# Scores and carried product on 64x64 quarters, and one written order for two stages, in a recurrent-attention and two-layer kernel

## The chip, the cores and the metric

One core of a Trainium2 chip runs the whole computation. The metric is device time in microseconds, the median of several executions of one program. Times inside an execution come from one profiled execution. Engines are called as the profile calls them: PE (matmul), PEld (weight load), DVE (vector), ACT (scalar), POOL, and SP, which here only issues DMAs.

## What is computed

Thirty-two heads (4 batches of 8) run a gated linear recurrence over 768 steps, and two dense layers follow on 3072 tokens.

```
for t in range(768):                                   # head dim 48
    state = alpha[:, :, t, :, None] * state + k[t] (outer) v[t]
    y[t]  = q[t] @ state
x   = y as (3072, 384)
h   = x @ w1_in ; x = max(0.01*h, h) @ w1_out          # d_ff 2048
h   = x @ w2_in ; out = elu(h) @ w2_out
```

## The kernel before

**Units.** The recurrence is cut into chunks of 128 steps. A unit is one chunk of one batch, all 8 heads as 4 pairs; there are 24, six in a row (c = u % 6) for each batch. The two heads of a pair lie at partitions 0 to 47 and 64 to 111. A unit makes, on PE in fp32 (each such product stands as two instructions in the trace): the scores `sc` (`attn_sc`, L171, lhsT of 48 rows by 128 columns, one bank for each half of the pairs), the transposed keys `pk` (L179), the output `po` from masked scores and values (L225, 128 rows by 64 or 48 columns), the carried product added to the same `po` (L231: the state `T`, 48 by 48, against the queries, only when c > 0), and the state update `pu` (L244, when c < 5). DVE masks the scores (L193), prepares keys and queries by two scans (`prep_k`, `prep_F`, `prep_q`), and adds the state (L268). `po` is then split in a high part `xh` (ACT, L250) and a low part `xl` (DVE, L253) of the x tile of a block.

**Blocks.** Four units make a block of 512 tokens. The fourth pair of a unit is spread over the free partitions of the other three pairs by six DMAs of 64 KiB on SP's queue (`gather`, L282) before the block can be used by layer 1. There are 6 blocks, and each of the two layers goes over 16 steps m for a block. A step is nine matmuls of `hp` (128x512, in a PSUM bank of `ps_h`, two banks), an activation on ACT and DVE, a split of the result in `gh` (ACT) and `gl` (DVE), and nine matmuls into `y` or `o`. The loop over `seq` issues, in step s, first `hp` of step s+2 (LA = 2) and its activation, then pieces of attention, then `y` of step s. `gh` and `gl` have two buffers, so that `gh` of step s+2 has to wait for the `y` of step s.

**Attention under layer 1.** Units 0 to 7 and the first heads of blocks 0 and 1 have an order written out by hand, up to step 16 (`in_order` ties each engine's instructions to program order). From there units 8 to 23 are handed out as pieces (`pieces`, four indices for a unit, index 0 `sc` and `pk`, index 1 the preparation of the next unit, index 2 `po` and `pu`) so that a block is complete in time for the next block of layer 1. From there on the order on each engine is the scheduler's (`behind` only keeps it after the part ordered by hand). After a unit's last piece the pack and values of unit u+3 are loaded by two DMAs of 674 and 288 KiB on ACT's queue (L116, L128).

**Layer 2's weights.** They come as 8-byte words and are converted in place over layer 1's weights by 32 conversions of four DVE and three ACT instructions (L290 to L302). All of them are asked for in the 16 steps of layer 1's last block. In layer 2, `guard_load` and `guard_unit` read the decay factors of every unit once more, and check on ACT that they are in range (L590, L594, L595).

`ps_a` has three banks that `sc` (two), `pk`, `po` and `pu` take in turn.

Of the kernel before, what the change touches and what calls it, by code (L numbers as in the profile page):

```python
# [19 lines left out]
def attention_two_layers_kernel(  # L20
# [17 lines left out]
    C = CHUNK  # L38
# [20 lines left out]
    ps_h = ctx.enter_context(tc.tile_pool(name="ps_h", bufs=2, space=PSUM))  # L59
# [10 lines left out]
    near = const.tile([1, 1], I32, name="near")  # L70

# [13 lines left out]
    def constants():  # L85
# [12 lines left out]
        nc.vector.memset(far_sum[:, 1:2], 1.0)  # L98


# [25 lines left out]
    def load_v(u, eng=None):  # L126
        t = v_p.tile([128, NP, 3 * D], F32, tag="v", name="vt")
        (eng or nc.sync).dma_start(t.rearrange("s p e -> s (p e)"), vals[u])  # L128
        vts[u] = t
# [73 lines left out]
    def attn_S(u):  # L203
        attn_sc(u)
        attn_pk(u)

    def attn_S_post(u):
        attn_mask(u)
        attn_kn(u)
        attn_T(u)  # L210

    def attn_V(u):
        attn_po(u)
        attn_pu(u)

    def attn_po(u):
# [4 lines left out]
        po = ps_a.tile([PR, NP, C], F32, tag="at", name="po")  # L221
        for p in range(NP):
            for j in range(2):
                wide = D if j else 64
                nc.tensor.matmul(po[64 * j:64 * j + wide, p], lhsT=vt[:, p, 2 * j * D:2 * j * D + wide], rhs=A[:, j, p],  # L225
                                 start=(p == 0), stop=(p == NP - 1 and c == 0), skip_group_check=True)
        if c > 0:
            for p in range(NP):
                for j in range(2):
                    r = slice(64 * j, 64 * j + D)  # L230
                    nc.tensor.matmul(po[r, p], lhsT=d["T"][r, p], rhs=qh[r, p],  # L231
                                     start=False, stop=(p == NP - 1), skip_group_check=True)
        d["po"] = po

    def attn_pu(u):
# [3 lines left out]
        if c < NC - 1:  # L239
            pu = ps_a.tile([PR, NP, D], F32, tag="at", name="pu")  # L240
            for p in range(NP):
                for j in range(2):
                    r = slice(64 * j, 64 * j + (D if j else 64))
                    nc.tensor.matmul(pu[r, p], lhsT=d["kn"][:, p, r],  # L244
                                     rhs=vt[:, p, 2 * j * D:(2 * j + 1) * D], start=(p == 0), stop=(p == NP - 1),
                                     skip_group_check=True)
            d["pu"] = pu

    def attn_xh(u, xh, off):
        nc.scalar.copy(xh[0:PR, :, off:off + C], st[u]["po"])  # L250

    def attn_xl(u, xh, xl, off):
        nc.vector.tensor_sub(xl[0:PR, :, off:off + C], st[u]["po"], xh[0:PR, :, off:off + C].bitcast(F32))  # L253

    def attn_rest(u, xh, off):
        nc.tensor.matmul(st[u]["po"], lhsT=minus, rhs=xh[0:PR, :, off:off + C], start=False, stop=True,
                         skip_group_check=True)

    def attn_xl_act(u, xl, off):
        nc.scalar.copy(xl[0:PR, :, off:off + C], st[u]["po"])  # L260
# [12 lines left out]
    def attn_V_post(u, xh, xl, off):  # L273
        attn_xh(u, xh, off)
        attn_xl(u, xh, xl, off)
        attn_state(u)
        st.pop(u)

    def gather(x, n, engs=None):
        for b in range(2 * KD):  # L280
            lo, hi = 64 * (b // 3) + 16 * (b % 3), 64 * (b % 2) + D
# [33 lines left out]
    def ffn1_h(j, m, ahead=0):  # L315
        xh, xl, n, _ = xt[j]
        hp = ps_h.tile([128, n], F32, tag="h", name="hp")
# [9 lines left out]
    def ffn1_t(j, m):  # L327
        t = g_p.tile([128, xt[j][2]], F32, tag="t", name="t")
        nc.scalar.activation(t, steps[1, j, m], ACTF.Copy, scale=0.01)  # L329
        steps[1, j, m] = t, steps[1, j, m]  # L330

    def ffn1_max(j, m):
        t, hp = steps[1, j, m]
        nc.vector.tensor_max(t, t, hp)  # L334

    def ffn1_gh(j, m):
        gh = gs_p.tile([128, xt[j][2]], F32R, tag="gh", name="gh")
        nc.scalar.copy(gh, steps[1, j, m][0])  # L338
        steps[1, j, m] = steps[1, j, m][0], gh
# [13 lines left out]
    FIRST = 4  # L353

# [27 lines left out]
    def x2_split(j):  # L382
        t = xs_p.tile([128, 2, KD + 1, 512], F32R, tag="x", name="x")
        xh, xl = t[:, 0], t[:, 1]
        for c in range(KD):
            split(xh[:, c], xl[:, c], x2t[j][:, c], nc.scalar)
        x2s[j] = xh, xl
# [3 lines left out]
    def ffn2_h(j, m):  # L391
        xh, xl = x2s[j]
        hp = ps_h.tile([128, 512], F32, tag="h", name="hp")
# [8 lines left out]
    def ffn2_g(j, m):  # L402
# [3 lines left out]
        nc.scalar.activation(t, t, ACTF.Exp, scale=-1.0)  # L406
        nc.vector.scalar_tensor_tensor(out=t, in0=t, scalar=-1.0, in1=hp, op0=ALU.add, op1=ALU.max)  # L407
# [602 lines left out]
```

## Time and profile before

| | us |
|---|---|
| median of 3 runs | 943.81 (941.28 to 947.72) |
| the profiled execution, its own time | 948.76 |
| its span, first to last instruction | 946.9 |
| PE busy | 914.9 (97%) |
| DVE busy | 533.5 (56%) |
| ACT busy | 447.5 (47%) |
| units 0 to 7, weights of layer 1, to 150 us | 150 |
| units 8 to 23 under layer 1, to 484.86 us | 334.9 |
| layer 1's last block, to 550.1 us | 65.2 |
| layer 2 | 396.8 |

Time is told from the span's start. In the timeline a row is a run of equal instructions merged: its start, the time to the end of the last one, the engine, line, operation, tiles and count; in brackets the idle time before it and what ended that. Since PE pipelines its matmuls, what a group costs is the time from its start to the start of the next group. A 128x512 matmul costs 0.227 us in this way, so nine of them 2.04 us.

### The profile page before, as it was taken

The page shows a single profiled execution, that of the slowest core. Times are in us where ns is not written, and L with a number is a line of the kernel's source. Part 1 is how long each engine was busy: PE and PEld are TensorE (multiplying, and loading weights), DVE is VectorE, ACT ScalarE, POOL GpSimd, SP SyncE. Part 2 cuts the span into 40 slices and gives each one's busy share as a digit, 9 for nine tenths or more (in the row PEclk, how much of TensorE's full clock was granted, in tenths as well). Part 3 has the DMA queues.
Part 4 walks back from the last instruction along what each step waited for, and adds up shares of the span by engine and source line. Part 5 has one row for each costly group of instructions (what it writes and reads, how often), then busy time and mean ns, then how long its engine had stood idle before and what let it go on. Part 6 is the DMA issues. An engine that isn't in the chain of part 4 may idle for free.

```text
span 946.9 us, 12777 instructions
## 1 busy us (share of the span) xinstructions
PE 914.9 (97%) x5027; PEld 744.0 (79%) x5027; DVE 533.5 (56%) x877; ACT 447.5 (47%) x784; POOL 1.1 (0%) x8
## 2 busy tenths in 40 slices
PE   7888999999999999999999999999999999999997
PEld 5665777787888788788888878878878878888896
DVE  7797779765555556554579974433433433333432
ACT  2445665222322323323467795564564565644443
POOL 0000000000000000000000000000000000000000
PEclk8899999999999999999999999999999999999999
DMA  9756342212122111212224520030210300300201
GB/s 243 200 154 164 106 128 67 85 43 59 42 84 60 42 43 42 59 43 82 74 81 117 152 64 10 11 73 1 35 48 1 64 20 0 64 1 1 34 1 37
DMA packets 54147, 62.35 MB, mean 66 GB/s; under 512 B 35328, under 2 KB 35840, under 8 KB 54080
## 3 DMA queue, kind: packets, MB, share of 16 engines
q1 hardware_dynamic: 50128, 48.03, 19.6%
q10 hardware_dynamic: 3952, 13.43, 5.0%
q8 instruction: 41, 0.67, 0.3%
q14 instruction: 26, 0.21, 0.1%
HBM read 54.37 MB, written 4.72 MB: 62 GB/s over the span
## 4 chain that ended last, share of the span: by engine, by line
PE 74%; DVE 10%; ACT 6%; DMA 6%; issue 2%; SPq 1%; ACTq 0%; DVEq 0%
PE hp L398 18%; PE y L367 15%; PE hp L323 15%; PE o L431 9%; PE oa L431 5%; PE oa L446 3%; PE po L225 2%; PE sc L171 2%; PE po L231 2%; DMA span<-in_seqs_dram 2%; DMA stg<-in_w_dram 2%; DMA x2t<-in_w_dram 1%; SPq L440 1%; DVE x2t L296 1%; DVE x2t L298 1%
## 5 line engine op out<-in xcount | busy, mean ns | idle before, releaser
L323 PE MATMUL hp<-x,w 128*128 128x512 f32 x864 | 213.7, 391 | 3.8 <-DMA x<-x 2.1
L398 PE MATMUL hp<-x,w 128*128 128x512 f32 x864 | 212.7, 390 | 3.4 <-DVE t L407 3.4
L323 PEld LDWEIGHTS hp<-x,w 128*128 128x128 f32 x864 | 161.5, 188 | 41.3 <-ACT w L299 2.5
L398 PEld LDWEIGHTS hp<-x,w 128*128 128x128 f32 x864 | 161.7, 188 | 37.7 <-DVE t L407 4.8
L367 PE MATMUL y<-gh,w 128*128 128x512 f32 x576 | 179.0, 399 | 3.6 <-ACT gh L338 3.0
L407 DVE SCALAR_TENSOR_TENSOR t<-t,hp 128x512 f32<-128x512 f32 x96 | 65.9, 686 | 149.9 <-ACT t L406 149.9
L367 PEld LDWEIGHTS y<-gh,w 128*128 128x128 f32 x576 | 106.5, 190 | 27.9 <-ACT gh L338 4.5
L367 PE MATMUL y<-gl,w 128*128 128x512 f32 x288 | 109.9, 397 | 1.0 <-DVE gl L344 1.0
L338 ACT CAST gh<-t 128x512 fp32r<-128x512 f32 x96 | 59.4, 620 | 108.7 <-PE y L367 59.5
L82 DVE TENSOR_TENSOR gl<-t,gh 128x512 fp32r<-128x512 f32 x96 | 66.3, 690 | 68.9 <-ACT gh L79 67.0
L329 ACT ACTIVATE t<-hp 128x512 f32<-128x512 f32 x96 | 56.9, 594 | 101.0 <-PE hp L323 100.7
L405 ACT ACTIVATE t<-hp 128x512 f32<-128x512 f32 x96 | 57.1, 595 | 90.7 <-PE hp L398 90.7
L334 DVE TENSOR_TENSOR t<-t,hp 128x512 f32<-128x512 f32 x96 | 65.2, 680 | 51.5 <-ACT t L329 51.5
L79 ACT CAST gh<-t 128x512 fp32r<-128x512 f32 x96 | 59.6, 621 | 71.4 <-PE o L431 22.6
L344 DVE TENSOR_TENSOR gl<-t,gh 128x512 fp32r<-128x512 f32 x96 | 66.0, 688 | 47.6 <-ACT gh L338 46.0
L431 PE MATMUL o<-gh,w 128*128 128x512 f32 x288 | 84.3, 390 | 0.3 <-ACT x2t L380 0.3
L367 PEld LDWEIGHTS y<-gl,w 128*128 128x128 f32 x288 | 54.5, 190 | 14.3 <-DVE gl L344 2.7
L431 PEld LDWEIGHTS o<-gh,w 128*128 128x128 f32 x288 | 53.9, 188 | 12.0 <-ACT x2t L380 0.9
L406 ACT ACTIVATE t<-t 128x512 f32<-128x512 f32 x96 | 60.6, 631 | 2.4
L431 PE MATMUL oa<-gh,w 128*128 128x512 f32 x192 | 56.5, 389 | 0.0
L431 PE MATMUL o<-gl,w 128*128 128x512 f32 x144 | 51.5, 389 | 0.0
L140 DVE TENSOR_TENSOR_SCAN E<-pack,d 112x517 f32<-112x517 f32 x23 | 28.3, 1232 | 25.6 <-DMA pack<-in_seqs_dram 25.6
(119 smaller groups left out, 888.7 us busy)
## 6 DMA issues: line engine op xcount, KB each, us to landing
stg<-in_w_dram SPq DMA_DIRECT2D x28, 384.0 KB, 3.2
pack<-in_seqs_dram ACTq DMA_DIRECT2D x13, 674.2 KB, 5.0
x2t<-in_w_dram SPq DMA_DIRECT2D x20, 384.0 KB, 3.4
span<-in_seqs_dram SPq DMA_DIRECT2D x24, 226.2 KB, 3.0
pack<-in_seqs_dram SPq DMA_DIRECT2D x8, 674.2 KB, 6.0
x2t<-in_w_dram SPq DMA_DIRECT2D x32, 144.0 KB, 2.7
out_dram<-osb SPq DMA_DIRECT2D x60, 64.0 KB, 2.0
vt<-in_vals_dram ACTq DMA_DIRECT2D x13, 288.0 KB, 5.3
```

Of the source, the lines that this page charges most:

```text
L79: nc.scalar.copy(dst, src)
L82: (lo_engine or nc.vector).tensor_sub(lo, src, dst.bitcast(F32))
L323: nc.tensor.matmul(hp, lhsT=a[:, kk, :], rhs=x[:, kk, :n], start=(i == 0), stop=(i == 3 * KD - 1))
L334: nc.vector.tensor_max(t, t, hp)
L338: nc.scalar.copy(gh, steps[1, j, m][0])
L344: nc.vector.tensor_sub(gl, t, gh.bitcast(F32))
L367: nc.tensor.matmul(ytiles[j][c], lhsT=a[:, c * 128:(c + 1) * 128], rhs=x, start=(first and i == 0), stop=(last and i == 2),)
L398: nc.tensor.matmul(hp, lhsT=a[:, kk, :], rhs=x[:, kk, :], start=(i == 0), stop=(i == 3 * KD - 1))
L405: nc.scalar.activation(t, hp, ACTF.Relu, scale=-1.0)
L406: nc.scalar.activation(t, t, ACTF.Exp, scale=-1.0)
L407: nc.vector.scalar_tensor_tensor(out=t, in0=t, scalar=-1.0, in1=hp, op0=ALU.add, op1=ALU.max)
L431: nc.tensor.matmul(otiles[j][c], lhsT=a[:, c * 128:(c + 1) * 128], rhs=x, start=(m == 0 and i == 0), stop=(m == KF - 1 and i == 2),)
```

## The change

Units 8 to 23 have three pieces. Piece 0 (`attn_scT`) makes the scores with 64-column halves of the keys, so that four products (two row halves, two column halves of the array) stand for two, and then the carried product into the output banks. In the carried product and in `po`, the two heads of the odd pairs are swapped, and the odd pairs have a bank of their own: `po` is two tiles, one in `ps_a` and one in `ps_h`. Layer 1 has the other `ps_h` bank alone as long as units run. `ffn1_t` copies `hp` out unscaled, and `ffn1_max` makes max(0.01 t, t) from the copy. Piece 1 is `pk`, piece 2 is `po` and `pu`. The carried state is made by `attn_carry` at the end of the unit before. The split is now three instructions on ACT and three on DVE for each unit. Pair 1 goes to `aside` and takes two more DMAs to its place in x, which `gather` issues as its third and fourth. The twelve pieces of a block come one in each of the steps m = 0 to 11.

Program order holds on every engine for all the rest (`in_order` at the end of each step, `behind` is gone). From layer 1's last block on, the steps are written out: `Flow` hands the 32 conversions out over 28 steps, so that they reach into layer 2's first block, and the splits of layer 2's inputs are spread over steps. The reduction that ends the guard stays in layer 2's fifth block, and its matmul moves behind that block's last `y`.

```diff
-    ps_h = ctx.enter_context(tc.tile_pool(name="ps_h", bufs=2, space=PSUM))
+    ps_h = ctx.enter_context(tc.tile_pool(name="ps_h", bufs=1, space=PSUM))
+    def hbank(n, name):
+        if not turn[1]:
+            turn[0] ^= 1
+        return ps_h.tile([128, n], F32, tag=f"h{turn[0] * (not turn[1])}", name=name)
...
+    def attn_carry(u):
+        d = st[u]
+        if u % NC > 0:
+            d["T"] = carried[:, 0:NP * D].rearrange("p (g e) -> p g e", e=D)
+            nc.vector.tensor_mul(d["T"], st["S"], d["pe"].to_broadcast([PR, NP, D]))
+
+    def attn_scT(u):
+        d = st[u]
+        kS, qh = d["kS"], d["qh"]
+        sc = [ps_a.tile([128, NP, C], F32, tag="at", name=f"sc{j}") for j in range(2)]
+        for p in range(NP):
+            for i in range(2):
+                for j in range(2):
+                    r, o = slice(64 * j, 64 * j + D), slice(64 * i, 64 * i + 64)
+                    nc.tensor.matmul(sc[j][o, p], lhsT=kS[r, p, o], rhs=qh[r, p, :], start=True, stop=True)
+        d["sc"] = sc
+        d["po"] = t = [ps_a.tile([PR, 2, C], F32, tag="at", name="po"), ps_h.tile([PR, 2, C], F32, tag="h1", name="po")]
+        if u % NC > 0:
+            for p in range(NP):
+                for j in range(2):
+                    o, dst = part(t, p, j)
+                    r = slice(64 * j, 64 * j + D)
+                    nc.tensor.matmul(dst, lhsT=carried[r, p * D:p * D + (D if o else 64)], rhs=qh[r, p],
+                                     start=(p < 2), stop=False, skip_group_check=True)
+
+    def part(t, p, j):
+        o = j ^ (p % len(t))
+        return o, t[p % len(t)][64 * o:64 * o + (D if o else 64), p // len(t)]
...
+    def outputs(u, x, i, off):
...
+        return [(t[0], x[0:PR, 0:NP:2, off:off + C]), (t[1][:, 0], aside()[0:PR, i, off:off + C]),
+                (t[1][:, 1], x[0:PR, NP - 1, off:off + C])]
...
+            if swapped and b == 2:
+                for j in range(2):
+                    nc.sync.dma_start(x[64 * j:64 * j + D, :, 1, :n].bitcast(F32),
+                                      aside()[64 - 64 * j:64 - 64 * j + D, :, :n].bitcast(F32))
...
-        nc.scalar.activation(t, steps[1, j, m], ACTF.Copy, scale=0.01)
+        nc.scalar.copy(t, steps[1, j, m])
-        nc.vector.tensor_max(t, t, hp)
+        nc.vector.scalar_tensor_tensor(out=t, in0=t, scalar=0.01, in1=t, op0=ALU.mult, op1=ALU.max)
...
     def attn_post(u, i):
+        last = u + 1 == NU
         if i == 0:
-            attn_S_post(u)
+            attn_mask(u)
+            if not last:
+                prep_k(u + 1)
         elif i == 1:
-            if u + 1 < NU:
-                attn_prep(u + 1)
-        elif i == 2:
+            attn_kn(u)
+            if not last:
+                prep_F(u + 1)
+                prep_q(u + 1)
+        else:
...
+            attn_xh(u, xh, off)
+            attn_state(u)
+            if not last:
+                attn_carry(u + 1)
+            attn_xl(u, xh, xl, off)
...
+                gather(t, blocks[j][1] * C, swapped=True)
             next_load(u + 3)
...
+                i, of = (s - KF + 1, KF - LA - 2) if s < 2 * KF else (m + 1, KF - LA - 2)
+            turn[1] = ph == 1 and j < NB - 1 and (s + LA) < (NB - 1) * KF
+            after = s - (NB - 1) * KF
+            if after >= 0:
+                quota = 4 * 33 * (after + 1) // PACE - flow.n if after < PACE else 0
...
+                    pe_h(n)
+                    f[0](n[1], n[2])
+                    flow.act(1)
+                    f[1](n[1], n[2])
+                    f[2](n[1], n[2])
+                    flow.act()
+                    flow.go(min(quota, 1))
+                    f[3](n[1], n[2])
+                (ffn1_y if ph == 1 else ffn2_y)(j, m)
...
+                flow.go(quota - 1)
+            else:
+                pe_h(n)
+                post_h(n)
+                for p in now:
+                    attn_pe(*p)
+                if m < KF - 1:
+                    for p in now:
+                        attn_post(*p)
+                ffn1_y(j, m)
...
+            in_order()
```

## Rows read from the trace of the kernel before

**Rows 1.** The page: the span, and part 1, busy us of each engine.

```profile
span 946.9 us, 12777 instructions
...
PE 914.9 (97%) x5027; PEld 744.0 (79%) x5027; DVE 533.5 (56%) x877; ACT 447.5 (47%) x784; POOL 1.1 (0%) x8
```

**Rows 2.** Busy time in four stages: stretch, length, PE, PEld, DVE, ACT, POOL, PEclk, DMA, GB/s.

```profile
0.00:150.00 150.00, 128.73 (x841) 98.19 (x841) 120.84 (x184) 74.11 (x113) 1.14 (x8) 0.93 0.60 162
150.00:484.86 334.86, 334.15 (x2157) 268.29 (x2158) 196.70 (x328) 109.07 (x189) 0.00 (x0) 1.00 0.20 57
484.86:550.10 65.24, 64.92 (x286) 53.34 (x286) 60.69 (x129) 51.51 (x107) 0.00 (x0) 1.00 0.44 128
550.10:946.90 396.80, 387.09 (x1746) 324.20 (x1744) 155.31 (x239) 212.81 (x378) 0.00 (x0) 1.00 0.12 27
```

**Rows 3.** PE's waits, 150 to 484.86 us: total us, times, longest.

```profile
PE hp L323 <- DMA x<-x: 0.6, 1, 0.6
```

**Rows 4.** PE's waits, 550.1 to 946.9 us.

```profile
PE hp L398 <- DVE t L407: 3.4, 4, 1.7
```

**Rows 5.** Timeline of PE: a unit with carried state, its two pieces and what follows.

```profile
249.90 1.16 PE L171 MATMUL sc<-pack 48*128 48x128 f32 x16
250.99 0.61 PE L179 MATMUL pk<-ident,pack 112*128 112x112 f32 x4
251.37 0.71 PE L367 MATMUL y<-gh,w 128*128 128x512 f32 x2
...
259.72 1.09 PE L225 MATMUL po<-A,vt 128*64 128x128 f32 x16
260.74 1.08 PE L231 MATMUL po<-pack,T 48*48 48x128 f32 x16
261.75 0.67 PE L244 MATMUL pu<-vt,kn 128*64 128x48 f32 x16
262.35 0.72 PE L367 MATMUL y<-gh,w 128*128 128x512 f32 x2
```

**Rows 6.** Timeline of PE: the same in a unit without carried state.

```profile
240.05 1.09 PE L225 MATMUL po<-A,vt 128*64 128x128 f32 x16
240.97 0.62 PE L244 MATMUL pu<-vt,kn 128*48 128x48 f32 x16
241.52 0.73 PE L367 MATMUL y<-gh,w 128*128 128x512 f32 x2
```

**Rows 7.** Timeline of ACT and DVE at the end of a step's `y`.

```profile
253.48 0.62 ACT L338 CAST gh<-t 128x512 fp32r<-128x512 f32 x1 [1.31 <-PE y L367]
...
254.14 0.69 DVE L344 TENSOR_TENSOR gl<-t,gh 128x512 fp32r<-128x512 f32 x1 [1.61 <-ACT gh L338]
```

**Rows 8.** Timeline of all engines: a block's last unit, to layer 1's next block.

```profile
381.68 0.32 ACTq L116 DMA_DIRECT2D pack<-in_seqs_dram  x1
...
382.22 1.21 ACTq L128 DMA_DIRECT2D vt<-in_vals_dram  x1
382.22 0.36 DVE L268 TENSOR_TENSOR S<-pu,T 112x192 f32<-112x192 f32 x1 [1.33 <-PE pu L244]
382.49 0.68 DVE L253 TENSOR_TENSOR x<-po,x 112x512 fp32r<-112x512 f32 x1
...
383.20 3.80 SPq L282 DMA_DIRECT2D x<-x  x6
...
391.10 1.60 PE L323 MATMUL hp<-x,w 128*128 128x512 f32 x6 [0.56 <-DMA x<-x]
```

**Rows 9.** Busy time of PE around a longer wait: stretch, length, PE, PEclk, DMA, GB/s.

```profile
87.87:91.00 3.13, 0.39 (x2) 1.00 1.04 246
91.92:95.33 3.41, 3.41 (x9) 0.50 0.65 160
```

**Rows 10.** The chain of waits in layer 2, around the end of its first block.

```profile
619.61 3.81 DMA span<-in_seqs_dram
...
627.50 0.53 ACT t L406
628.03 0.02 issue
628.05 0.70 DVE t L407
...
628.79 2.34 PE hp L398 x9
```

More of the change, by code (lines that the diff above doesn't have):

```diff
@@ L220, in attn_po @@
         A, qh = d["A"], d["qh"]
-        po = ps_a.tile([PR, NP, C], F32, tag="at", name="po")
+        if u < UB + blocks[1][1]:
+            d["po"] = [ps_a.tile([PR, NP, C], F32, tag="at", name="po")]
+        t = d["po"]
+        n = len(t)
         for p in range(NP):
             for j in range(2):
[L224 to L227, printed above, removed]
+                o, dst = part(t, p, j)
+                c0, wide = (3 * p + 2 * j) * D, D if o or (n == 2 and c > 0) else 64
+                nc.tensor.matmul(dst[0:wide], lhsT=vt[:, c0:c0 + wide], rhs=A[:, j, p],
+                                 start=(p < n and (n == 1 or c == 0)), stop=(p >= NP - n and (n == 2 or c == 0)),
+                                 skip_group_check=True)
+        if c > 0 and n == 1:
             for p in range(NP):
@@ L380, in ffn1_y, with x2_split @@
                     nc.scalar.copy(dst[:, c], ytiles[j][c])
[L382 to L387, printed above, removed]
+    def x2_split(j, c):
+        if c == 0:
+            t = xs_p.tile([128, 2, KD + 1, 512], F32R, tag="x", name="x")
+            x2s[j] = t[:, 0], t[:, 1]
+        xh, xl = x2s[j]
+        split(xh[:, c], xl[:, c], x2t[j][:, c], nc.scalar)
     x2s = {}
@@ L555, in attention_two_layers_kernel, with __init__ @@
     class Conversions:
-        def __init__(self, layer, order):
-            self.layer, self.order = layer, order
+        def __init__(self, order):
+            self.order = order
             self.done = [0, 0, 0]
@@ L572, in a @@
                 m = self.order[i][1]
-                if self.layer == 1 and m >= 2 and m + 2 < KF:
+                if m >= 2 and m + 2 < KF:
                     stage1(m + 2)
-                if self.layer == 2:
-                    slots2.append(staged[(2,) + self.order[i]])
-                    fill2()
         def b(self, upto):
@@ L673, in general @@
         for j in range(NT // 512):
-            x2_split(j)
+            for c in range(KD):
+                x2_split(j, c)
             for m in range(KF):
@@ L693, in in_order @@
         traced[0] = len(ins)
-    def behind():
-        ins = list(nc.cur_bb.bb.instructions)
-        last = {x.engine: x for x in ins[:traced[0]]}
-        for x in ins[traced[0]:]:
-            if x.engine in last:
-                tc.add_manual_dep(
-                    x, last[x.engine].name,
-                    mybir.DependencyInfo(mybir.DependencyClass.NoSync, mybir.DependencyReason.DATA),
-                    reason="behind")
     with ExitStack():
@@ L858, in post_h @@
             (ffn1_g if e[0] == 1 else ffn2_g)(e[1], e[2])
-        pieces = [(u, i) for u in range(UB + blocks[1][1], NU) for i in range(4)]
+        pieces = [(u, i) for u in range(UB + blocks[1][1], NU) for i in range(3)]
         for s, e in enumerate(seq):
@@ L921, in attention_two_layers_kernel @@
                 if u == NU:
-                    guard()
-        behind()
+                    nc.vector.tensor_reduce(out=far_sum[:, 0:1], in_=outside, axis=AX.X, op=ALU.add)
+            in_order()
         with tc.If(nc.values_load(near, min_val=0, max_val=1) == 0):
```

204 lines of the change are left out of this document (133 added, 71 removed).

## The prediction

> **What bounds the kernel now.** I read the page's first part first: PE is busy in 914.9 of 946.9 us [rows 1]. A busy PE alone says little, so I cut the span into stages [rows 2]. Only the first 150 us, where weights are converted and which the change leaves alone, show PE idle for long. From 150 us on PE waits for nothing worth a line: under the units its longest wait is 0.6 us [rows 3], and layer 2 loses 3.4 us in four waits [rows 4]. So from 150 us on the time is the sum of PE's instructions, and a change can gain in two ways: fewer microseconds of PE work, or those few waits. It can lose in every way that makes PE wait, since there is no slack to lose it in.
>
> What the units cost PE is read from the timeline, from the start of one group to the start of the next. For a unit with carried state: scores 250.99 - 249.90 = 1.09, transposes 0.38, `po` 1.02, carried product 1.01, `pu` 0.60, together 4.10 us [rows 5]. Without the carried product between them `po` and `pu` take 0.92 and 0.55 [rows 6]. Thus each change of the array's shape costs some 0.1 us.
>
> **Part 1, quarters.** The scores are 16 instructions in 1.09 us, 0.068 us each; one that went alone through its 128 columns in two passes could not be so quick, since four transposes of 112 columns take 0.095 each [rows 5]. So the two halves of the array run side by side, each with 8 instructions, and take about 0.92 / 8 = 0.115 us for one [rows 6]. The carried product has the same pace, 1.01 us for 16 [rows 5], although it occupies only two quarters. New: the scores are 32 instructions over four quarters, again 8 for each, so nothing is gained there. The carried product has 16 over four, 4 for each, where it was 8. If the four run side by side, piece 0 takes 12 x 0.115 + 0.1 for the change of shape = 1.5 us, against 1.09 + 1.01 = 2.10: 0.6 less. `po` and `pu` then follow each other without a change of shape, 1.47 for 1.62: 0.15 less. But the transposes stand alone in a step, and piece 0 gets a way back to the full array of its own: 0.15 more. Net 0.6 for each unit with c > 0; of units 8 to 23 these are 14: **-8.4 us**. The two units with c = 0 keep their price.
>
> No row shows four quarters at work, so the bounds are wide. If two quarters that share rows run one after the other, each half of the array has 24 instructions: 24 x 0.115 + 0.1 = 2.86, 0.76 more than now; 14 of these and two units with 16 per half (0.85 more each) are +12.3 us. I take the gain: `po` (column halves) and the scores (row halves) both overlap in these rows, and the quarters need both at once.
>
> A rule speaks against it. The Trainium skill (TensorE: Matmul & The Clock Gate, "Wait — 56ns, not 53.3ns?") says that the sequencer can need about 62 ns for each matmul, which binds when the work of one is shorter. The 48 instructions of piece 0 would then take 3.0 us (an estimate from that page) and the change would lose. `pu` shows 16 in 0.60 us, 0.037 each [rows 5]: the rule does not hold at this place.
>
> **Part 2, one bank for `hp`.** It costs nothing as long as ACT's copy is done before PE returns to the bank: 0.6 us of copy lie beside the 2.04 of `y`. If ACT came late by over 1.4 us, every step would pay.
>
> **Part 3, program order under the units.** `gh` of a step starts when that step's `y` ends (253.48, and the next `hp` starts at 253.51), and `gl` ends 1.32 us after that [rows 7]. In program order everything that DVE does for a piece is now behind this `gl`. Let Y be the end of `y` in a step with piece 2. State and carry are 192 columns, 0.36 each, less with overlap (the next starts 0.27 after) [rows 8]: done at Y + 1.9. The low part of `po` took 0.68 for 512 columns [rows 8]; as 256, 128 and 128 I put 0.42, 0.28 and 0.28, the first done at Y + 2.2, the last at Y + 2.65. The next unit's scores want the `ps_a` bank that the first of these frees, at Y + 2.04 + 0.1 after the next `hp`. So PE waits about 0.1 us at 11 units (after c = 5 the banks fall otherwise): **+1.1 us**, between 0 and 0.5 for each unit. The carried state is needed after the scores and is ready. DVE's load holds: a unit's three steps are 16.5 us for PE and some 11 for DVE.
>
> **Part 4, the gather.** Here something gets late. Now the six DMAs start at 383.20, 1.5 us behind the loads of pack and values, and `hp` of the next block has to wait for them until 391.10: 7.9 us [rows 8]. New: they start at Y + 2.7, since the last low part comes behind `y`, `gh`, `gl`, state and carry. The last piece is at m = 11 and the block's first `hp` stands in step 14, behind two steps of 4.08: Y + 8.16. That leaves 5.5 us. ACT starts the loads at about Y + 1.2, so they again go 1.5 us ahead. The wait is then 7.9 - 5.5 = 2.4, and two DMAs of 48 rows, three times as large as the others, come in the middle. The other boundaries can be better off: the wait of 0.6 is the only one at `hp` [rows 3], and after c = 5 there is no state, 0.7 us less. I put 2.5 us for the three boundaries with unit loads and nothing for the last, where no unit is loaded (8 issues of 3.80 / 6 = 0.63 fit [rows 8]). 7.5 less the wait of now, 0.6: **+6.9 us**, between -0.6 and +12.
>
> **Part 5, last block and layer 2.** Layer 2's waits are ACT's: a batch of guard work stands ahead of the activation, its DMA lands after 3.81 us, and `hp` waits for DVE behind it [rows 10]. In program order each `guard_unit` is two steps (8.2 us) behind its load, so these waits go: **-3.4 us**. The conversions move off a stage where DVE is busy 60.7 of 65.2 us [rows 2]. There an instruction is 60.69 / 129 = 0.47. New per step: 132 / 28 = 4.7 of them and two of about 0.65, some 3.5 of 4.08 us, with some idle time before `gl` filled by the one conversion instruction that `Flow` puts there. Two steps also hold guard work on ACT, but `gh` is needed two steps later. I put 0, up to +4 if DVE's in-order waits add up. The gate's matmul and the three splits of layer 2's input are small, 0.
>
> **Sum.** -8.4 + 1.1 + 6.9 - 3.4 = -3.8 us against the profiled execution of 948.76, that is 945.0. That execution was 5 us above the median of 943.81; on the median the same sum gives **940 us**.
>
> **Rivals.**
> *The gather is hidden.* If the DMAs land 2.4 us sooner, Part 4 turns to -0.6 and the sum to -11.3: 932.5. For it: at three of four boundaries nothing waits now [rows 3]. Against: the start moves later by what those have to spare. 0.22.
> *The quarters do not run side by side* (for shared rows, or by the sequencer's rule). +12.3 for -8.4, so 943.8 + 12.3 + 1.1 + 6.9 - 3.4 = 961. Against: overlap in rows 5. It decides when piece 0 takes over 2.7 us. 0.09.
> *The gather costs the clock.* A wait of 3.13 us was followed by 3.41 us at half clock [rows 9], 1.7 us lost. If the three boundaries pass that length, say 4 us, they cost 3 x 5.7 = 17.1 in place of 7.5: +5.8 in all, 949.6, slower than before. For it: 2.4 is near, and the two large DMAs are not in it. Against: these can come in two shorter waits. It decides from about 3 us of one wait. 0.18.
>
> **How the numbers follow.** My forecast has 0.5: 940, by itself 934 to 946. About 0.01 is left for what I don't see. About 1% (9.4 us) is what a measurement of this kernel can tell from no change, so faster means below 934.4 and slower above 953.2. Faster: two thirds of the first rival and a tenth of the forecast, 0.20. Slower: the second rival and a sixth of the third, 0.12. Same: 0.68. The range for 8 in 10 goes from the first rival to the third, 931 to 951.
>
> **What will show it.** Piece 0: 48 instructions in about 1.5 us (2.9 if the second rival holds). `po` followed at once by `pu` in 1.5. A wait of `hp` for the x DMAs at blocks 2 to 4 of some 2.5 us each, and PEclk 1.00 behind it (0.50 in the third rival). Waits of the scores' first instruction for DVE of about 0.1. No waits for DVE `t` in layer 2, and none in the 28 steps of `Flow`. Wrong above all if the gather lands in time, or if PE waits inside the steps for ACT or DVE.

## The result, and the profile after

The changed kernel takes 935.55 us (median of 6 runs, 932.19 to 937.80), the kernel before 944.12 beside it (6 runs, 941.28 to 947.72). The ratio is 0.990, with a 95% interval of 0.987 to 0.993. That is 8.6 us less, about 1%, and the interval stays clear of 1. It lies below the forecast of 940 and inside its range of 931 to 951.

The page of the changed kernel, span and busy time of each engine, answers to [rows 1]. PE is busy for 16.9 us less, although it has 256 instructions more. Of these, 6.2 us lie in the first stage below, whose work is the same, and go with the clock:

```profile
span 933.4 us, 13414 instructions
...
PE 898.0 (96%) x5283; PEld 732.0 (78%) x5283; DVE 542.7 (58%) x909; ACT 449.9 (48%) x816; POOL 1.4 (0%) x11
```

Busy time by stages, first of the kernel before, then of the changed one. Both are cut at the same work, counted in 128x512 matmuls (18 for a step): at the start of steps 17, 20, 80, 112 and 176. Columns as in [rows 2].

```profile
0.00:147.00 147.00, 126.08 (x831) 96.50 (x832) 118.29 (x181) 71.78 (x109) 1.14 (x8) 0.93 0.61 164
147.00:164.83 17.83, 17.33 (x123) 13.25 (x121) 16.77 (x27) 8.18 (x14) 0.00 (x0) 1.00 0.18 60
164.83:476.53 311.70, 311.14 (x2009) 249.81 (x2009) 176.35 (x292) 98.16 (x169) 0.00 (x0) 1.00 0.21 58
476.53:607.78 131.25, 130.93 (x577) 107.94 (x576) 96.98 (x192) 94.22 (x187) 0.00 (x0) 1.00 0.26 74
607.78:873.59 265.81, 262.42 (x1155) 216.02 (x1154) 100.58 (x152) 145.76 (x258) 0.00 (x0) 1.00 0.14 28
873.59:946.90 73.31, 66.99 (x337) 60.50 (x335) 24.57 (x37) 29.39 (x48) 0.00 (x0) 0.99 0.11 23
```

```profile
0.00:142.10 142.10, 119.90 (x832) 91.86 (x832) 118.20 (x181) 71.63 (x109) 1.19 (x9) 0.98 0.63 169
142.10:162.35 20.25, 18.49 (x140) 14.02 (x139) 15.15 (x23) 7.76 (x13) 0.00 (x0) 0.92 0.04 15
162.35:465.88 303.53, 299.95 (x2250) 241.48 (x2249) 177.64 (x316) 89.39 (x185) 0.22 (x2) 1.00 0.24 63
465.88:597.03 131.15, 131.08 (x578) 107.97 (x577) 103.78 (x199) 98.36 (x196) 0.00 (x0) 1.00 0.30 85
597.03:858.15 261.12, 261.12 (x1154) 216.22 (x1153) 103.27 (x153) 152.04 (x265) 0.00 (x0) 1.00 0.14 30
858.15:933.40 75.25, 67.45 (x339) 60.44 (x337) 24.67 (x39) 30.74 (x51) 0.00 (x0) 0.97 0.10 23
```

Read the lengths line against line. The first stage is 4.9 us shorter, with the same work in the same order. Its column PEclk says why: 0.93 against 0.98. The clock stood at 0.50 for 20.5 us of it before (16.83 to 30.48, and 3.41 us each from 68.03 and from 91.92), for 6.8 us after (3.41 us each from 17.72 and from 85.98). The change has no part in it: the second run of the scores on halves, a variant of the changed kernel, also has 20.5 us at 0.50 and takes 147.5 us for this stage, and the kernel before takes 142.2 us in the run with the written order alone, with 13.7 us at 0.50. This is why the two profiled spans differ by 13.5 us and the medians by 8.6. Take the 4.9 off and the stages give what the medians give: hand-over +2.4, the steps with units -8.2, layer 1's last block with layer 2's first -0.1, layer 2's blocks two to five -4.7, the rest +1.9, in all -8.6.

**The steps with units.** From the timeline of PE, added up from the start of each group to the start of the next, for steps 20 to 79 (15 units, 9 to 23):

| us | before | after |
|---|---|---|
| scores | 18.02 (240 instructions) | 14.21 (480) |
| carried product (13 units) | 13.17 (208) | 7.08 (208) |
| transposes (12 units) | 4.59 | 4.06 |
| `po` from masked scores | 15.31 | 13.98 |
| `pu` (12 units) | 6.85 | 6.54 |
| what a 128x512 matmul takes over its 0.227 beside a small group | 7.11 (37 groups) | 7.37 (42 groups) |
| `hp` waits for a gather | 0.73 | 2.40 |
| `pk` waits for the mask | 0 | 1.82 |
| sum | 65.78 | 57.46 |

So 12.1 us left PE's small products, and 3.8 us came back as waits and neighbours. The waits are counted from start to start here; the view of waits below counts from the end of a matmul's record and gives 1.9 for the 2.40. One unit of the changed kernel on PE's timeline, which answers to [rows 5]:

```profile
182.36 1.11 PE L228 MATMUL sc<-pack 48*64 48x128 f32 x32
183.29 0.62 PE L236 MATMUL po<-pack,carried 48*64 48x128 f32 x16
183.84 0.73 PE L410 MATMUL y<-gh,w 128*128 128x512 f32 x2
...
188.08 0.57 PE L190 MATMUL pk<-ident,pack 112*128 112x112 f32 x4
188.42 0.71 PE L410 MATMUL y<-gh,w 128*128 128x512 f32 x2
...
192.69 1.08 PE L256 MATMUL po<-A,vt 128*48 128x128 f32 x16
193.61 0.61 PE L275 MATMUL pu<-vt,kn 128*64 128x48 f32 x16
194.15 0.73 PE L410 MATMUL y<-gh,w 128*128 128x512 f32 x2
```

Piece 0 goes from 182.36 to 183.84, 1.48 us for 48 instructions; the scores take 0.93, twice the instructions in less time than before. `po` and `pu` take 0.92 and 0.54.

PE's waits in 160 to 470 us (total us, times, longest), which answers to [rows 3]:

```profile
PE hp L365 <- DMA x<-x: 1.9, 3, 0.9
PE pk L190 <- DVE A L204: 1.7, 1, 1.7
```

From 535 us to the end the same view is empty: the waits of [rows 4] are gone. No wait for the one `hp` bank and none of the scores for a bank stands in either.

**A block boundary.** All engines at the end of block 2's last unit, which answers to [rows 8]; piece 2 belongs to the step whose `y` ends at 292.26:

```profile
292.24 0.62 ACT L380 CAST gh<-t 128x512 fp32r<-128x512 f32 x1 [2.91 <-PE y L410]
292.26 2.20 PE L365 MATMUL hp<-x,w 128*128 128x512 f32 x9
292.30 0.32 ACTq L125 DMA_DIRECT2D pack<-in_seqs_dram  x1
...
292.76 0.36 ACT L292 CAST x<-po 112x256 fp32r<-112x256 f32 x1
...
295.12 1.22 SPq L324 DMA_DIRECT2D x<-x  x2
...
296.38 1.25 SPq L320 DMA_DIRECT2D x<-x2t  x2
...
297.68 2.66 SPq L324 DMA_DIRECT2D x<-x  x4
...
300.42 0.84 PE L365 MATMUL hp<-x,w 128*128 128x512 f32 x3
...
302.16 1.63 PE L365 MATMUL hp<-x,w 128*128 128x512 f32 x6 [0.89 <-DMA x<-x]
```

The load of the pack is issued at 292.30, ahead of ACT's copy at 292.76 that stands before it in the program, and 2.8 us ahead of the gather at 295.12. `hp` begins at 300.42 in time (the first DMAs landed at 299.84 and 300.09) and waits 0.89 us behind its third matmul, for the large DMAs of pair 1, which landed at 300.72 and 301.47, and those behind them.

### The profile page after: what moved, and what is told of

It is laid out like the page before. It is cut to its first block, busy times and chain, and to the rows that moved or that the text cites. A ratio compares the mean times of both kernels' runs of the same rounds, so it can differ in the third digit from the quotient of the medians.

```text
span 933.4 us, 13414 instructions
## 1 busy us (share of the span) xinstructions
PE 898.0 (96%) x5283; PEld 732.0 (78%) x5283; DVE 542.7 (58%) x909; ACT 449.9 (48%) x816; POOL 1.4 (0%) x11
## 4 chain that ended last, share of the span: by engine, by line
PE 83%; DVE 8%; ACT 3%; DMA 3%; SPq 1%; issue 1%; ACTq 0%; DVEq 0%
PE hp L441 21%; PE y L410 18%; PE hp L365 16%; PE o L490 11%; PE oa L490 7%; PE oa L505 3%; PE po L256 2%; PE sc L228 2%; DVE x2t L338 1%; DMA x2t<-in_w_dram 1%; DVE x2t L340 1%; DMA x<-x 1%; PE o L505 1%; DVE E L151 1%; PE pu L275 1%
## 5 line engine op out<-in xcount | busy, mean ns | idle before, releaser
L410 PE MATMUL y<-gh,w 128*128 128x512 f32 x576 | 184.4, 401 | 3.6 <-ACT gh L380 2.9
L410 PE MATMUL y<-gl,w 128*128 128x512 f32 x288 | 113.3, 393 | 1.0 <-DVE gl L386 1.0
L371 ACT COPY t<-hp 128x512 f32<-128x512 f32 x96 | 56.2, 586 | 100.0 <-PE hp L365 99.9
L448 ACT ACTIVATE t<-hp 128x512 f32<-128x512 f32 x96 | 57.3, 597 | 81.3 <-PE hp L441 81.3
L490 PE MATMUL o<-gh,w 128*128 128x512 f32 x288 | 88.8, 389 | 0.1
L376 DVE SCALAR_TENSOR_TENSOR t<-t 128x512 f32<-128x512 f32 x96 | 66.0, 687 | 37.8 <-ACT t L371 35.7
L490 PE MATMUL oa<-gh,w 128*128 128x512 f32 x192 | 59.1, 389 | 0.0
L490 PE MATMUL o<-gl,w 128*128 128x512 f32 x144 | 56.0, 389 | 0.0
L490 PEld LDWEIGHTS oa<-gh,w 128*128 128x128 f32 x192 | 36.0, 188 | 7.5
```

The costliest lines, as they stand in the source:

```text
L376: nc.vector.scalar_tensor_tensor(out=t, in0=t, scalar=0.01, in1=t, op0=ALU.mult, op1=ALU.max)
L410: nc.tensor.matmul(ytiles[j][c], lhsT=a[:, c * 128:(c + 1) * 128], rhs=x, start=(first and i == 0), stop=(last and i == 2),)
L448: nc.scalar.activation(t, hp, ACTF.Relu, scale=-1.0)
L490: nc.tensor.matmul(otiles[j][c], lhsT=a[:, c * 128:(c + 1) * 128], rhs=x, start=(m == 0 and i == 0), stop=(m == KF - 1 and i == 2),)
```

## The experiments

No experiment leaves out a part of the computation. Kernels run on one chip shared the runs of the kernel before (945.49 us for the first four, 945.34 for the next four, 945.61 for the last two). "Steps 20 to 79" is the length of the third stage above: 311.70 before, 303.53 changed.

### Scores on halves again

```diff
         for p in range(NP):
-            for i in range(2):
-                for j in range(2):
-                    r, o = slice(64 * j, 64 * j + D), slice(64 * i, 64 * i + 64)
-                    nc.tensor.matmul(sc[j][o, p], lhsT=kS[r, p, o], rhs=qh[r, p, :], start=True, stop=True)
+            for j in range(2):
+                r = slice(64 * j, 64 * j + D)
+                nc.tensor.matmul(sc[j][:, p], lhsT=kS[r, p, :], rhs=qh[r, p, :], start=True, stop=True)
```

> The changed kernel with one thing undone: the scores of units 8 to 23 are again 8 products of 128 columns on two row halves, and the carried product stays on four quarters. Theory: the quarters do not make the scores quicker by themselves (8 instructions for each part of the array in both shapes), they only spare a change of shape ahead of the carried product and part of the start. Then scores and carried product together take 1.65 to 1.75 us instead of 1.48, and the kernel takes 16 x 0.2 = 3 us more than the changed one (about 939). Rival: the shape of the scores is of no account, the gain over the kernel before (1.20 us on average) came from pieces that are no longer split: piece 0 stays at 1.48, same time as the changed kernel (935.5). Second rival: quarters are quicker for each instruction; then the scores alone take over 1.15 and the loss is 4 us or more.

Measured: 935.85 us, ratio 0.990 [0.988, 0.992], steps 20 to 79 306.37 (+2.8). PE's timeline of the unit above:

```profile
181.88 1.16 PE L227 MATMUL sc<-pack 48*128 48x128 f32 x16
182.97 0.67 PE L235 MATMUL po<-pack,carried 48*64 48x128 f32 x16
183.57 0.73 PE L409 MATMUL y<-gh,w 128*128 128x512 f32 x2
```

Piece 0 takes 1.69 us: 1.09 and 0.60 where quarters take 0.93 and 0.55. Over the stage the scores take 16.38 against 14.21 us and the carried product 7.77 against 7.08, 2.9 us together. The starts of single instructions in the two traces say where the 0.16 us of the scores come from. One round, two instructions on halves or four on quarters, follows the other by about 0.11 us in both. With halves the second round comes 0.21 us behind the first instead of 0.16, and the carried product 0.21 us behind the last round instead of 0.11. So the quarters have no better pace for the scores; they spare a change of shape and part of the start, as the theory said. The whole time does not show it here. The pair was run again, side by side, in five rounds: the changed kernel as it is, and the scores on halves.

> The changed kernel itself, on one chip with the next run, as the base for it: ratio to the kernel before 0.988 to 0.993, steps 20 to 80 in 303.5 us of the profile.

> The scores on two row halves once more, beside the changed kernel on one chip. The profile of the earlier run had 2.8 us more in steps 20 to 80, the times of that run did not show it. Theory: the 2.8 us are real: steps 20 to 80 take 306.4 again and the ratio to the kernel before is 0.003 above that of the changed kernel beside it. Rival: the loss is given back elsewhere (waits of the gather get shorter as the steps get longer): the ratios agree within 0.001.

Measured: 937.12 us, 0.990 [0.986, 0.993], and 938.34 us, 0.992 [0.990, 0.995]. The intervals overlap, so the time does not settle it. The profiles of this pair have scores of 14.24 and 16.37 us, the same 2.1 apart, but steps 20 to 79 are only 1.2 apart (303.71 and 304.90): with halves, `hp` waited 0.3 us for gathers in that execution, and 1.7 with quarters. The gain in PE's work is shown; in the profiles 1.2 and 2.8 us of it are left in the length of the stage, and what is left in the time is not shown.

### The pairs not swapped

```diff
-        o = j ^ (p % len(t))
+        o = j
...
-        return [(t[0], x[0:PR, 0:NP:2, off:off + C]), (t[1][:, 0], aside()[0:PR, i, off:off + C]),
-                (t[1][:, 1], x[0:PR, NP - 1, off:off + C])]
+        return [(t[0], x[0:PR, 0:NP:2, off:off + C]), (t[1], x[0:PR, 1:NP:2, off:off + C])]
...
-                gather(t, blocks[j][1] * C, swapped=True)
+                gather(t, blocks[j][1] * C)
```

The carried product then has two quarters of the array instead of four, and the two large DMAs of pair 1 fall away.

> The changed kernel with the swap undone: head j of every pair stays on quarter (j, j), so the carried product uses two quarters, the pairs go straight to x, the two large DMAs through the spare tile and the third part of the split are gone. Theory: four quarters at work are what makes the carried product quick: it goes from 0.55 back to 0.9 to 1.0 us, 14 x 0.4 = 5.6 us lost; the waits of hp for the x DMAs (0.42 + 1.05 + 0.93 us) go away with the large DMAs, 2.4 won; about 3 us slower than the changed kernel (938.5 to 939.5). Rival: the carried product is quick because it follows the scores without a change of shape, not because of four quarters: it stays near 0.55 and the kernel gains 2.4 us (933).

Measured: 937.15 us, 0.993 [0.990, 0.996], steps 20 to 79 306.71 (+3.2). The same unit on PE's timeline:

```profile
182.58 1.11 PE L228 MATMUL sc<-pack 48*64 48x128 f32 x32
183.51 1.06 PE L236 MATMUL po<-pack,carried 48*64 48x128 f32 x16
184.50 0.72 PE L409 MATMUL y<-gh,w 128*128 128x512 f32 x2
```

The carried product costs 0.99 instead of 0.55, over the stage 12.83 instead of 7.08 us (+5.75), and no `hp` waits for a gather any more (-2.4). The difference, 3.3, is what the stage shows, near the 3 us of the theory; the interval of the time overlaps that of the changed kernel. This is the heart of the change: four quarters against two, at the price of two larger DMAs at each boundary.

### The loads closer to the gather

```diff
-    def load_unit(u, first=False, eng=None):
+    def load_unit(u, first=False, eng=None, held=False):
         t = pack_p.tile([PR, EXT + 2 * NP * C], F32, tag="pack", name="pack")
+        if held:
+            nc.scalar.copy(t[:, 0:1], bias[:, 0:1])
...
-            load_unit(u, eng=nc.scalar)
+            load_unit(u, eng=nc.scalar, held=u % 4 == 2)
```

One small copy into the new pack keeps its load behind ACT's copies at a boundary, so that it starts where the prediction had put it, 1.5 us ahead of the gather.

> The changed kernel, with the unit loads at three block ends held back: a copy of one column into the new buffer stands behind the high part on ACT, and the load has to wait for it, so that it starts about 1.4 us ahead of the gather (as the prediction had it) instead of 2.8. Theory: what a gather waits for is the load ahead of it, so its head start sets the wait; the waits of hp at these three boundaries grow by about 1.3 us each, from 2.4 to 6 us in all, and the kernel takes 939 to 940 (the clock could fall behind such a wait and add to it). Rival: the two large DMAs and the issue rate of 0.63 us set the wait; it stays at 2.4 and the time at 935.5.

Measured: 941.64 us, 0.996 [0.994, 0.998], steps 20 to 79 308.07 (+4.5). PE's waits in 150 to 480 us, the one for the x tile; and one boundary on the timeline:

```profile
PE hp L367 <- DMA x<-x: 5.6, 5, 1.4
```

```profile
296.55 0.32 ACTq L127 DMA_DIRECT2D pack<-in_seqs_dram  x1
...
298.08 1.22 SPq L326 DMA_DIRECT2D x<-x  x2
...
304.39 0.94 PE L367 MATMUL hp<-x,w 128*128 128x512 f32 x3 [0.83 <-DMA x<-x]
```

The load starts 1.5 us ahead of the gather (296.55, 298.08), and now the first matmul of `hp` waits too. Counted against undisturbed matmuls the boundaries lose 6.7 us, against 2.4 with the loads 2.8 us ahead. It confirms the mechanism of the gather as predicted: the closer the loads stand ahead of it, the later it lands.

### The loads behind the gather

```diff
+            eng = nc.sync if u % 4 == 2 else nc.scalar
-            load_unit(u, eng=nc.scalar)
-            load_v(u, eng=nc.scalar)
+            load_unit(u, eng=eng)
+            load_v(u, eng=eng)
```

> The changed kernel, with the unit loads at the three block ends issued on SP's queue behind the gather. Theory (the load ahead sets the wait): the eight DMAs then land as at the last boundary, where nothing was loaded and the last one landed 6.9 us after the first issue; waits of 0.42 + 1.05 + 0.93 go down to at most 0.3 each, the kernel gains 1.5 to 2.4 us over the changed one (933 to 934). Rival: issue rate and large DMAs set the wait: waits stay, 935.5. The load itself is used two units later, some 30 us, so nothing should wait for it.

Measured: 937.07 us, 0.992 [0.989, 0.994], steps 20 to 79 302.12 (-1.4). PE's waits for the x tile in 150 to 470 us:

```profile
PE hp L365 <- DMA x<-x: 0.2, 1, 0.2
```

Some 0.6 us of loss at the boundaries is left of 2.4. The profile shows it; the time cannot be told from that of the changed kernel. What delays the gather is the 962 KiB of pack and values on the way at the same time. The landings in the traces say so too: at the nine boundaries with both loads ahead (three each of the kernel before, of the changed one and of the held loads) the first DMA of the gather landed 0.2 to 0.6 us after the later of the two loads, whatever its own start; here it lands 2.3 us after its issue. The two large DMAs have their part as well, since with the pairs not swapped no `hp` waits although the loads go ahead as before.

### The written order alone, under the units

The kernel before, with program order on every engine for the steps with units, and the pieces moved by as many steps as that needs.

```diff
-                i, of = (s - KF, KF - LA - 1) if s < 2 * KF else (m + 1, KF - LA)
+                i, of = (s - KF, KF - LA - 2) if s < 2 * KF else (m + 1, KF - LA - 2)
...
+            if s < (NB - 1) * KF - LA:
+                in_order()
         behind()
```

> The kernel before, with program order on every engine in the steps of units 8 to 23 (as in the changed kernel) and the pieces of a block handed out in twelve steps; shapes, banks and splits as before. Theory: the order alone gains what the scheduler lost by splitting pieces (scores 1.20 us in the mean against 1.09 in one piece, transposes 0.38 against 0.34): 2 to 3 us in steps 20 to 80 (311.7 in the kernel before, 303.5 in the changed one), so about 309, and the rest of the 8 us is the quarters'. Rival: program order puts the units' work behind gl and costs waits of PE, 312 or more, and the quarters gain more than the changed kernel shows. In time: 941 to 943 against 944 to 945.5 of the kernel before.

Measured: 952.70 us, 1.008 [1.005, 1.011], steps 20 to 79 313.87 (+2.2). Again a unit on PE's timeline, its `po`:

```profile
255.84 1.52 PE L225 MATMUL po<-A,vt 128*64 128x128 f32 x16
257.29 1.08 PE L231 MATMUL po<-pack,T 48*48 48x128 f32 x16
```

Two things happen in these steps. The groups are no longer split, 30 of them instead of 37: the scores take 16.39 instead of 18.02 us, and their neighbours 6.1 instead of 7.1. But `po` takes 20.76 instead of 15.31 us: in every one of the 15 units its weight load waits up to 0.3 us for DVE's mask, which stands only one step before. In the changed kernel, with two steps between mask and `po`, no such wait stands. Most of the loss in time lies elsewhere: steps 17 to 19 take 22.85 instead of 17.83 us, with 3.41 us at a clock of 0.50 (1.7 us lost) and `hp` waiting for converted weights. So the rival came true, and the order by itself loses.

### The quarters without the written order

The changed kernel, with the scheduler's order for the steps 17 to 79.

```diff
+                if s >= (NB - 1) * KF:
+                    in_order()
+                elif s == (NB - 1) * KF - 1:
+                    behind()
-            in_order()
```

> The changed kernel with the order of the steps of units 8 to 23 left to the scheduler (program order again from layer 1's last block on). Theory: quarters keep their prices, but pieces are split again and the scheduler brings waits of its own: steps 20 to 80 take 305 to 307 us instead of 303.5, the kernel 2 to 4 us more (938 to 940). Rival: order is of no account here or harmful, since it holds the waits of 1.8 us for the mask and 2.4 us for the gather: then 299 to 302 and a time of 932 to 934.

Measured: 968.21 us, 1.024 [1.021, 1.028], steps 20 to 79 333.75 (+30.2). PE's timeline around one piece 0:

```profile
239.60 0.66 PE L228 MATMUL sc<-pack 48*64 48x128 f32 x8
240.19 2.34 PE L365 MATMUL hp<-x,w 128*128 128x512 f32 x9
242.46 0.44 PE L228 MATMUL sc<-pack 48*64 48x128 f32 x4
242.83 1.66 PE L410 MATMUL y<-gh,w 128*128 128x512 f32 x6
244.41 0.44 PE L228 MATMUL sc<-pack 48*64 48x128 f32 x4
```

The scores are dealt out in groups of 4 to 8 between the large matmuls. A group of four costs 0.37 us where it costs 0.12 inside a run of 32. There are 105 small groups instead of 42; their neighbours lose 20.5 us instead of 7.4, and the groups themselves cost more: scores 22.06 instead of 14.21 (though 26 of their 480 instructions lie ahead of these steps), carried product 10.43 instead of 7.08, `po` 19.39 instead of 13.98. Neither of the sizes that were expected was near. This run says what the written order is for: not to remove waits, but to keep the small products together.

### Program order in layer 2 alone

The kernel before, with program order from layer 2's first step on.

```diff
         for s, e in enumerate(seq):
             ph, j, m = e
+            if ph == 2 and j == 0 and m == 0:
+                behind()
+                traced[0] = len(list(nc.cur_bb.bb.instructions))
...
+            if ph == 2:
+                in_order()
-        behind()
```

> The kernel before, with program order on every engine in layer 2 only. Theory: layer 2's waits come from guard work that the scheduler put ahead of the activations in batches; in program order they go, and blocks 2 to 5 of layer 2 (step 112 to 176) take 261.1 us as in the changed kernel instead of 265.8: 4 to 5 us less in all (940 against 945). Rival: the waits come from the load of ACT and the DMA itself, or went because the changed kernel spreads the splits of layer 2's inputs; then 264 to 266 stay.

Measured: 947.47 us, 1.002 [1.000, 1.004]. PE's waits from 500 us on:

```profile
PE hp L398 <- DVE t L407: 2.9, 1, 2.9
PE pf L600 <- DVE far_sum L598: 2.4, 1, 2.4
```

The expected 940 did not come. The four waits of the guard are gone and blocks two to five take 2.0 us less, 263.8, but two new waits stand: at 553.56 us PE waits for conversions that layer 1's last block did not finish (3.1 us, and then 3.4 us at a clock of 0.50; steps 80 to 111 take 4.2 us more), and at 872.57 the guard's matmul waits 2.4 us for its reduction; without that wait the blocks would be near the 261.1 of the changed kernel. The change avoids just these two, by handing the conversions out over 28 steps and by moving that matmul behind the block's last `y`. That `Flow` costs nothing is so by its cover, not by its nature.

### Both late places mended

The loads behind the gather, as above, and DVE's mask ahead of the three additions at a block's last step.

```diff
+                else:
+                    for u, i in now:
+                        if i == 0:
+                            attn_mask(u)
                 ffn1_y(j, m)
                 if m == KF - 1:
-                    for p in now:
-                        attn_post(*p)
+                    for u, i in now:
+                        if i == 0:
+                            prep_k(u + 1)
+                        else:
+                            attn_post(u, i)
```

> The changed kernel with the loads at three block ends behind the gather, as in the earlier run, and with the mask of the piece in block 0's last step ahead of the three additions of y (the transposes of step 20 waited 1.82 us for that mask). Theory: 1.4 to 1.8 us from the gather and about 1 us of the 1.82 (the additions come later and y waits a little for its bank): 2.5 us less than the changed kernel, ratio to the kernel before 0.987 to 0.988. Rival: the wait moves to y in full, then 0.989 to 0.990.

Measured: 932.58 us, 0.987 [0.984, 0.989], steps 20 to 79 301.0 (-2.5). The wait of the transposes for the mask is no longer a line of PE's waits (all transposes of the stage together take 0.8 us more than the changed kernel's did apart from that wait), a new one of 0.5 us of `y` for the additions stands beside it, and the boundaries lose 0.7. The ratio is what the theory said. It has the lowest median of the kernels that were run; its interval overlaps that of the changed kernel.

## Why the prediction was right or wrong

**Right in kind, 4.8 us too cautious.** The forecast of 940 us, within 1%, holds the outcome; the sum was -3.8 and the profiles, without the chance of the first stage, give -8.6. Some of the closeness is luck: the quarters, the gather and layer 2 came out 10.5 us better than their terms (4.0, 5.2 and 1.3), and the hand-over, the end and a wait for the mask gave some 5 back. Both signs of being wrong that were named came in part: the gather landed nearly in time, and PE waited for DVE inside a step.

**Part 1, quarters: right in mechanism, mis-sized.** Piece 0 was to take 1.5 us and takes 1.48; `po` and `pu` together were to take 1.47 and take 1.46. So the pace of 0.115 us for one instruction in its quarter holds, and the four do work side by side. The term -8.4 (of which 7.8 for the 13 units with a carried state of these steps) came out as -11.8 there (-12.1 and +0.3 of neighbours). Two steps of it failed. The price before was read off one unit of [rows 5], 1.09 for the scores, but the scheduler had split them in some units: 18.02 / 15 = 1.20 on the mean. And the transposes' own way back to the full array, put at 0.15 for each unit, costs almost nothing beyond before, since the split scores had paid for such ways already (37 groups before, not 30; 42 after, not 45). "Nothing is gained there" holds for the pace of the scores; the 0.93 against 1.09 is the start and the change of shape that the first experiment shows, and the 1.5 for piece 0, with one change of shape for its 12 rounds, already had it.

**Part 2: right.** No wait for the `hp` bank; 0.

**Part 3: wrong by 1.1.** No wait of the scores for a bank was seen. But a wait that had not been seen coming took more than its place: piece 0 of one unit stands in the last step of a block, and there DVE has three additions of `y` to the output (1.88 us) ahead of the mask. DVE and PE in the changed kernel at that place:

```profile
168.76 0.69 DVE L386 TENSOR_TENSOR gl<-t,gh 128x512 fp32r<-128x512 f32 x1 [2.87 <-ACT gh L380]
169.37 1.88 DVE L419 TENSOR_TENSOR x2t<-y,x2t 128x512 f32<-128x512 f32 x3
171.16 1.28 DVE L204 TENSOR_TENSOR A<-sc,causal 128x512 f32<-128x512 f32 x2
171.99 0.57 PE L190 MATMUL pk<-ident,pack 112*128 112x112 f32 x4 [1.66 <-DVE A L204]
```

The mask begins when the additions end, and the transposes, which take a bank that the mask frees, stand behind it: 1.8 us. The prediction had named what stands behind `gl` in an ordinary step and left out the step in which a block ends.

**Part 4, the gather: the term that was wrong most, +6.9 said, +1.7 measured.** By its steps: the gather was to start at Y + 2.7, and starts at Y + 2.86 (295.12 - 292.26). `hp` was to need it at Y + 8.16, and does (300.42). What failed is "ACT starts the loads at about Y + 1.2, so they again go 1.5 us ahead": they start at Y + 0.04, since ACT's queue sent the transfer ahead of the copies that stand before it in the program. With 2.8 us of lead for the loads the gather's first DMAs land in time. The held loads show the counterpart: put where the prediction had them, the boundaries lose 6.7 us, near the 7.5 of the prediction, and the kernel takes 941.6, near its 940. So the mechanism was sound and one start time was not; it had been argued from where the loads stand in the program, not from a row. The wait of 7.9 us was also read at the slowest boundary: from the pack's issue to the landing of the values it is 8.9 us there, and 6.4 to 7.0 us in the changed kernel. The third rival (a wait long enough to cost the clock) stayed away at the boundaries: the longest wait is 0.9 us, and PEclk is 1.00 from 162 to 466 us.

**Part 5: right, a little small.** -3.4 was said for the guard's waits and blocks two to five are 4.7 shorter. The term was mis-sized because the 3.4 of [rows 4] is idle time, counted from the end of a matmul's record. From start to start the same four places, at 628, 694, 761 and 828 us, lose 0.7, 1.2, 1.9 and 0.8 us against undisturbed matmuls, together 4.7, and the changed kernel has none. `Flow` costs nothing: steps 80 to 111 are as long as before, 131.15 against 131.25, and the run with program order in layer 2 alone shows what they would cost without it.

**Not in the sum: the hand-over, +2.4, and the rest, +1.9.** In the hand-over the clock falls to 0.50 once more. PE's timeline of the changed kernel ahead of it, and the busy time of the stretch, columns as above:

```profile
149.61 0.51 PE L365 MATMUL hp<-x,w 128*128 128x512 f32 x1 [0.77 <-ACT w L341]
150.60 3.60 PE L365 MATMUL hp<-x,w 128*128 128x512 f32 x8 [0.49 <-DVE w L344]
```

```profile
150.84:154.25 3.41, 3.41 (x10) 2.52 (x10) 3.34 (x7) 0.01 (x1) 0.00 (x0) 0.50 0.00 0
```

Ahead of it `hp` waits for weights that ACT and DVE convert, 0.77 and 0.49 us here and 0.50 us at 145.24. So the clock fell behind waits far shorter than the 3 us of one wait from which the third rival was to decide. These waits do not decide it alone either: the run with the loads behind the gather has 0.75 and 0.49 us at this place, and no fall. It and two more with the same order (pairs not swapped, and the second run of the scores on halves) had no such stretch and took 18.7 us for steps 17 to 19, not 20.2. So some 1.6 us of the +2.4 comes and goes, and what decides it is open. The kernel before does not have the wait of 0.77 for ACT there; it may be the other 0.8 us, which no run tests. The rest at the end, +1.5 behind the last step and +0.5 before, differs from run to run by as much as that and was not followed.

## What to carry to other kernels

Small products that share PE with large ones are priced by the row and by the number of groups: 32 quarter products in one run cost 0.93 us, and 0.37 for every four when they are dealt out, so keep them together by a written order before counting what the quarters save. Program order on every engine makes late work somebody's wait, so list for each step, the last one of a block included, what stands ahead of the work that PE needs next. Where transfers meet, read when each is issued from a row: 1.3 us more or less between a large load and a small gather was worth 4 us over three boundaries here.

## What the runs showed of the hardware

**Four quarters at once.** 32 instructions of 48 rows by 64 columns went through in 0.93 us, 0.029 us each, and 16 in 0.55. In the unit shown the four of a round, one for each quarter, start 5 to 8 ns apart, and the next round some 0.11 us later (182.52, 182.63, 182.75). The Trainium skill (TensorE: Matmul & The Clock Gate, "Wait — 56ns, not 53.3ns?") names about 62 ns for each matmul as a bound of the sequencer with hardware decode off, and a floor of about 25 ns between starts; the trace goes by neither (0.029 us on the mean stands in place of the first, 5 to 8 ns between neighbours in place of the second). Which setting of the decoder these runs had, no row tells.

**Two row halves in one bank.** The carried product of the kernel before writes with both row halves of the array to the same bank, at other partitions. 16 instructions take 1.01 us, where one half after the other would be 16 times 0.115, 1.84 (an estimate from the pace in the prediction), and the two of a pair start 6 to 8 ns apart. The Trainium skill (TensorEngine Tiling (Array Packing), "Gotcha 1: PSUM Pressure") says that different row tiles can't access the same bank at the same time; these rows don't agree with it.

**A change of shape** costs the large matmul ahead of a small group 0.07 us and the one behind it 0.10 (3.01 / 41 and 4.36 / 42), and much the same where there are 105 (0.09 and 0.11; 9.1 and 11.4 us in all). The Trainium skill (TensorEngine Tiling (Array Packing), "Key Properties") says that a change of the tiling mode drains the array; it gives no time. The extra time here fits with that; no row shows the drain itself.

**A DMA on ACT's queue runs ahead of ACT's copies**: issued at 292.30, before a copy at 292.76 that precedes it in the program order that the kernel asks for. All 13 unit loads of the changed kernel from 160 us on go so, each 0.01 to 0.12 us after `gh` of its step starts and 0.4 to 0.5 us before the first of the three copies. None goes ahead of that `gh`, which had itself waited; so the place in the program may still hold a load, and no row tells what does.
